# The second product of the larger experts with the weights stationary: output formed transposed, then turned over by transposes

## Chip, core and metric

One core of one Trainium2 chip runs the whole program. The metric is device time in microseconds (us) of one execution, lower is better. Engines are named as in the profile: PE (TensorE matmul), PEld (its weight loads), DVE (VectorE), ACT (ScalarE), POOL (GpSimd), SP (SyncE, which issues most of the DMAs).

## What is computed

An attention-like recurrence, a gated MLP, and a mixture of eight experts in which each of 3072 tokens goes to one expert. The change is in the last part:

```python
expert_idx = np.argmax(logits, axis=1)
gate_w = probs[np.arange(N), expert_idx]
for e in range(E):                       # E = 8, D = 384, F = 1024
    mask = expert_idx == e
    h = np.maximum(x[mask] @ w1[e], 0.0)
    out[mask] = gate_w[mask, None] * (h @ w2[e])
```

## The kernel before

The first 620 us compute the recurrence, the MLP and the routing. Each token's row (384 values, logits, its number) is scattered into `xs`, a region of slots for each expert. The last 245 us, the expert phase, is what the change touches.

Experts are taken by falling size. `CAPS` gives the slots of each: 448, 480, 448, 432, 416, 400, 384, 372. `tiles[e]` cuts them into row tiles: four when there are more than 384 slots (experts 0 to 5), else three. An expert has `XF` = 8 steps f, one for each 128 rows of the hidden layer. Every product is made of three matmuls on a high and a low part of the operands (32-bit data in a matmul format of reduced precision).

- `load_rows(e)` (L1168) brings the expert's rows from `xs` to `xrow`, by a DMA on SP. Its pool `xrp` has three buffers, so the load of expert e+2 takes the buffer of expert e-1. It is written into step 2 of expert e.
- `do_xT(e, k)` turns the rows into columns: transposes into a bank of `ps_t` (two banks), then a copy on ACT and a difference on DVE into `xk`.
- `load_we` and `split_we` bring the weights of one step (`wraw`, 384 KB, three buffers) by a DMA on SP and split them into `we`, high part on ACT (L816), low part on DVE (L819). `weights(e, f)` splits those of step f of the next expert and issues the load of the step two further on. `follow` keeps a split behind the last `relu` in `last_relu` in ACT's order.
- `emit_h(e, f)` (L1198): nine matmuls `ph` with the weights stationary and all slots as moving columns, into one of two banks; then `relu`: ACT (L902) and DVE (L903) write `ht`.
- `emit_y(e, f, t)` (L1211): for row tile t three matmuls `y` with the tile's columns of `ht` stationary (100 to 128 of them) and 384 columns of weights moving, summed over the eight steps into bank t of `ps_y`.
- `finish(e, t)` (L1222): the tile times its gate, on ACT for even t and on DVE for odd t, into `yo`, and a scatter by POOL (L1228) to the rows of `out` that `xrow` names. So the buffer `xrow` of an expert is free when its last scatter has landed.
- `drain2` (L1283) keeps `emit_y` two steps (`LAG`) behind `emit_h`: step 7 of expert e is drained in step 1 of expert e+1, and its tiles are finished there.

Expert 0 is treated apart (L1245 to L1279): its first 336 rows have been through `first_h` by then, and the last 112 go through short 32-bit matmuls (L1258) and `relu` into `h0`, between its `emit_y`.

The engines' queues run in order; a scheduler that works from its own estimates sets the order on each when the program is built, and an instruction waits in its queue for what it needs.

Of the kernel before, what the change touches and what calls it, by code (L numbers as in the profile page):

```python
# [8 lines left out]
F32 = mybir.dt.float32  # L9
# [5 lines left out]
AF = mybir.ActivationFunctionType  # L15
# [8 lines left out]
CAPS = (448, 480, 448, 432, 416, 400, 384, 372)  # L24
# [31 lines left out]
def kernel(  # L56
# [14 lines left out]
    nc = tc.nc  # L71
    P = 128
    NCH = att.shape[0]
    NT, DM = out.shape
# [5 lines left out]
    XF = 8  # L80
# [4 lines left out]
    wp = wstk.enter_context(tc.tile_pool(name="wp", bufs=18))  # L85
# [8 lines left out]
    def distinct_rows(key, ins):  # L94
        ins = getattr(ins, "ins", ins)
        tc.declare_no_dep(ins, group=key, reason="scatters of distinct rows")
        tc.add_to_no_dep_group(key, ins)
        scatters.setdefault(key, []).append(ins)
# [24 lines left out]
    def wtile(nm):  # L123
        return wp.tile([P, 1568], F32R, tag="w", name=nm)
# [169 lines left out]
    if True:  # L294
        ident = cst.tile([P, P], F32, name="ident")
# [159 lines left out]
        for i in range(7):  # L455
            n = 1 << i
# [4 lines left out]
        pt = ps_a.tile([P, 4, P], F32, tag="a0", name="pt")  # L461
# [339 lines left out]
        we = {}  # L801
# [9 lines left out]
        last_relu = []  # L811
# [81 lines left out]
        def products(ph, w, x):  # L893
            n = 0
            for k in range(3):
                wh, wl = w[:, k * P:(k + 1) * P], w[:, 768 + k * P:768 + (k + 1) * P]
                for a, b in ((wh, 0), (wh, 1), (wl, 0)):
                    nc.tensor.matmul(ph, a, x[:, k, b, :], start=(n == 0), stop=(n == 8))  # L898
                    n += 1

        def relu(ht, ph):
            q = nc.scalar.activation(ht[:, 0, :], ph, AF.Relu)  # L902
            nc.vector.scalar_tensor_tensor(ht[:, 1, :], ph, 0.0, ht[:, 0, :], op0=ALU.max, op1=ALU.subtract)  # L903
            return q
# [165 lines left out]
        while threads:  # L1070
            th = min((t for t in threads if met(t[3])), key=lambda t: t[0])
            now, t0, dt, need, name, gen = th
# [82 lines left out]
        ps_t = ph2.enter_context(tc.tile_pool(name="ps_t", bufs=2, space=bass.MemoryType.PSUM))  # L1155
        ps_y = ph2.enter_context(tc.tile_pool(name="ps_y", bufs=1, space=bass.MemoryType.PSUM))
# [3 lines left out]
        xk = {}  # L1160
        gate = {}
        hts = {}
        yo = {}


        tiles = [(c // (3 if c <= 3 * P else 4), 3 if c <= 3 * P else 4) for c in CAPS]

        def load_rows(e):  # L1168
            st, n = tiles[e]
            t = xrp.tile([st, n, RW], F32, tag="xrow", name="xrow", padded_shape=[P, 4, RW])  # L1170
            q = nc.sync.dma_start(
                out=t, in_=xs[bass.ds(at[e] * REGION, CAPS[e])].rearrange("(t p) c -> p t c", p=st)
            )
            after_scatters("xs", q)

            follow(getattr(q, "ins", q), last_we[0])
            xrow[e] = [t[:, i] for i in range(n)]
            xcol[e] = t[:, :, 384:393]

        def do_xT(e, k):  # L1180
            if k == 0:
                if e % 2 == 0:
                    t = r2p.tile([P, 3072], F32R, tag="r2", name="xk")
                else:
                    t = x2p.tile([P, 6 * REGION], F32R, tag="xk", name="xk")
                xk[e] = t[:, 0:6 * CAPS[e]].rearrange("p (k l n) -> p k l n", k=3, l=2)
            pt = ps_t.tile([P, CAPS[e]], F32, tag="t", name="pt2", padded_shape=[P, 512])
            st, n = tiles[e]
            for t in range(n):
                nc.tensor.transpose(pt[:, t * st:(t + 1) * st], xrow[e][t][:, k * P:(k + 1) * P], ident[:st, :st])  # L1190
            nc.scalar.activation(xk[e][:, k, 0, :], pt, AF.Copy)
            nc.vector.tensor_tensor(xk[e][:, k, 1, :], pt, xk[e][:, k, 0, :], op=ALU.subtract)

        def do_gate(e, after=None):
            x = xcol[e]
            gate[e] = gates(gp, *tiles[e], x[:, :, 0:E], x[:, :, E], after)

        def emit_h(e, f):  # L1198
            n = CAPS[e]
            ph = ps_h.tile([P, n], F32, tag="h", name="ph", padded_shape=[P, 512])  # L1200
            products(ph, we[e, f], xk[e])
            if e < E - 1:
                ht = hp.tile([P, 2 * REGION], F32R, tag="ht", name="ht")
            else:
                ht = wtile("ht")
            ht = ht[:, 0:2 * n].rearrange("p (l n) -> p l n", l=2)
            last_relu.append(relu(ht, ph))
            st, n = tiles[e]
            hts[e, f] = [ht[:, :, t * st:(t + 1) * st] for t in range(n)]

        def emit_y(e, f, t):  # L1211
            w = we[e, f]
            wh, wl = w[:, 384:768], w[:, 1152:1536]
            ht = hts[e, f][t]
            if f == 0:
                yo[e, t] = ps_y.tile([tiles[e][0], DM], F32, tag=f"y{t}", name=f"y{t}", padded_shape=[P, 512])
            for n, (a, b) in enumerate(((0, wh), (0, wl), (1, wh))):
                nc.tensor.matmul(  # L1218
                    yo[e, t], ht[:, a, :], b, start=(f == 0 and n == 0), stop=(f == XF - 1 and n == 2)
                )  # L1220

        def finish(e, t):  # L1222
            o = yp.tile([tiles[e][0], DM], F32, tag="yo", name="yo", padded_shape=[P, DM])
            if t % 2 == 0:
                nc.scalar.activation(o, yo[e, t], AF.Copy, scale=gate[e][:, t:t + 1])  # L1225
            else:
                nc.vector.tensor_scalar(o, yo[e, t], gate[e][:, t:t + 1], None, op0=ALU.mult)
            q = nc.gpsimd.indirect_dma_start(  # L1228
                out=out, out_offset=bass.IndirectOffsetOnAxis(ap=xrow[e][t].bitcast(I32)[:, 393:394], axis=0),
                in_=o, in_offset=None, bounds_check=NT - 1, oob_is_err=False,  # L1230
            )
            distinct_rows("out", q)
# [3 lines left out]
        def weights(e, f):  # L1236

            if e + 1 < E:
                n = (e + 1) * XF + f
                split_we(*todo[n])  # L1240
                if n + 2 < len(todo):
                    load_we(*todo[n + 2])
# [8 lines left out]
        pt = ps_t.tile([P, 3, ST], F32, tag="t", name="pt0")  # L1251
# [3 lines left out]
        for f in range(XF):  # L1255
            ph = ps_h.tile([P, ST], F32, tag="h", name="ph0")
            for k in range(3):
                nc.tensor.matmul(  # L1258
                    ph, fst["w", f // 4][:, f % 4, k * P:(k + 1) * P], x0T[:, k, :], start=(k == 0), stop=(k == 2)
                )  # L1260
            h0_done = relu(h0[:, f], ph)
            hm = fst["h", f // 2][:, f % 2]
            hts[0, f] = [hm[:, :, t * ST:(t + 1) * ST] for t in range(3)] + [h0[:, f]]
        c0 = fp.tile([ST, NST, 9], F32, name="c0")
# [3 lines left out]
        for f in range(XF):  # L1268
            for t in range(NST):
                emit_y(0, f, t)  # L1270
            weights(0, f)
            if 3 <= f < 6:
                do_xT(1, f - 3)
            elif f == 6:
                do_gate(0, h0_done if FIRST_AFTER else None)
                do_gate(1, h0_done if FIRST_AFTER else None)
                load_rows(2)
# [5 lines left out]
        def drain2(n):  # L1283
            while len(pend) > n:
                e, f = pend.pop(0)
                for t in range(tiles[e][1]):
                    emit_y(e, f, t)
                    if f == XF - 1:
                        finish(e, t)

        for e in range(1, E):
            for f in range(XF):
                emit_h(e, f)
                if e < E - 1:
                    pend.append((e, f))
                    weights(e, f)
                    if 3 <= f < 6:
                        do_xT(e + 1, f - 3)
                    elif f == 6:
                        do_gate(e + 1, last_relu[-1] if GATE_AFTER else None)  # L1300
                drain2(LAG)
                if f == 2 and e + 2 < E:
                    load_rows(e + 2)
        drain2(0)
        for t in range(tiles[E - 1][1]):
            for f in range(XF):
                emit_y(E - 1, f, t)
            finish(E - 1, t)
# [86 lines left out]
```

## Time and profile before

| | us |
|---|---|
| median of three runs (877.1 to 884.46) | 882.45 |
| profiled execution, its own time | 879.17 |
| its span, first to last instruction | 877.5 |
| expert phase in it: expert 0 up to the first `emit_h` of expert 1 | 618 to 653.1 |
| experts 1 to 7 | 653.1 to 864.8 |

The profiled execution is 3.3 us under the median of the runs. The profile lists busy time by engine, the chain of work that ended last, groups of instructions by line, and, by stretch of time, what each engine did and which clock TensorE was granted (1.00 is 2.4 GHz, 0.50 is 1.2 GHz). In a timeline a row merges like instructions: start, busy time, engine, line, operation, output and inputs, shape, count, and in brackets the idle time before it and what ended that.

### The profile page before, as it was taken

The numbers are of one execution on the slowest core, as the hardware profiler recorded it, in microseconds if no ns is written. First come the engines' busy times: TensorE is split into PE (matmuls) and PEld (weight loads), VectorE is DVE, ScalarE is ACT, GpSimd is POOL, SyncE is SP. The second block draws the span as 40 slices with busy tenths as digits, with TensorE's granted clock in tenths as the row PEclk, the third lists the DMA queues.
The fourth block names the chain that finished last, engine by engine and source line by source line (L and its number), as shares of the span: only waits on it lengthen the run. The fifth ranks groups of instructions, "written<-read, shape, count | busy, mean of one in ns | idle before, by whom it ended". The sixth has DMA issues, their size and how long they took to land.

```text
span 877.5 us, 13439 instructions
## 1 busy us (share of the span) xinstructions
PE 840.9 (96%) x5217; PEld 765.8 (87%) x5217; DVE 469.0 (53%) x950; ACT 328.3 (37%) x657; POOL 268.8 (31%) x297
## 2 busy tenths in 40 slices
PE   6898999899999999999999999999899999999994
PEld 5787988788888888888888888888899999999994
DVE  8988985645436444545455424343465554554640
ACT  4554543322224222422242214233354454453540
POOL 5504036755344634363435210200110201110111
PEclk9798999999999999999999999999999999999997
DMA  8716463222121212131213001520554445434401
GB/s 339 300 70 223 152 234 118 64 92 64 56 64 66 90 55 64 55 101 55 64 55 102 1 10 40 186 73 18 154 147 145 128 130 166 148 114 124 149 18 34
DMA packets 31865, 93.53 MB, mean 107 GB/s; under 512 B 4694, under 2 KB 15162, under 8 KB 28850
## 3 DMA queue, kind: packets, MB, share of 16 engines
q1 hardware_dynamic: 25010, 80.98, 27.5%
q0 software_dynamic: 6784, 11.61, 4.7%
q8 instruction: 43, 0.70, 0.3%
q14 instruction: 28, 0.23, 0.1%
HBM read 74.82 MB, written 16.25 MB: 104 GB/s over the span
## 4 chain that ended last, share of the span: by engine, by line
PE 82%; DVE 7%; issue 5%; ACT 2%; DMA 1%; POOL 1%; SPq 0%; POOLq 0%; ACTq 0%; DVEq 0%
PE o L750 18%; PE pgate L707 14%; PE pval L707 14%; PE y L1218 11%; PE ph L898 9%; PE pgv L707 4%; PE py L623 3%; PE pa L600 2%; PE py L619 2%; PE pg L431 1%; DVE x L401 1%; POOL out_dram L1228 1%; DVE x L402 1%; PE pt L1190 1%; DVE gt L739 1%
## 5 line engine op out<-in xcount | busy, mean ns | idle before, releaser
L707 PE MATMUL pgate<-xt,gv 128*128 128x512 f32 x540 | 136.0, 395 | 0.0
L707 PE MATMUL pval<-xt,gv 128*128 128x512 f32 x540 | 134.2, 393 | 0.0
L720 DVE TENSOR_TENSOR sgw<-pval,sgw 128x512 f32<-128x512 f32 x60 | 41.5, 691 | 162.1 <-PE pval L707 151.4
L750 PE MATMUL o<-wo,gth 128*128 128x392 f32 x480 | 126.6, 345 | 0.0
L707 PEld LDWEIGHTS pval<-xt,gv 128*128 128x128 f32 x540 | 100.3, 188 | 21.3
L1218 PE MATMUL y<-we,ht 128*120 128x384 f32 (+6 forms) x624 | 118.4, 339 | 0.0
L707 PEld LDWEIGHTS pgate<-xt,gv 128*128 128x128 f32 x540 | 100.8, 189 | 18.3
L898 PE MATMUL ph<-xk,we 128*128 128x336 f32 (+7 forms) x576 | 116.1, 349 | 0.0
L1218 PEld LDWEIGHTS y<-we,ht 128*120 128x120 f32 (+6 forms) x624 | 106.0, 175 | 2.6
L898 PEld LDWEIGHTS ph<-xk,we 128*128 128x128 f32 x576 | 102.7, 188 | 3.8 <-DVE ht L903 0.2
L561 POOL TENSOR_TENSOR Am<-ident,sd 128x1024 f32<-128x1024 f32 (+3 forms) x21 | 38.6, 1838 | 172.6 <-PE py L623 166.4
L716 ACT ACTIVATE sgw<-pgate 128x512 f32<-128x512 f32 x60 | 36.1, 601 | 141.6 <-PE pgate L707 141.6
L750 PEld LDWEIGHTS o<-wo,gth 128*128 128x128 f32 x480 | 85.8, 188 | 3.2 <-issue 0.5
L1228 POOL DMA_INDIRECT out_dram<-yo,xrow x26 | 28.7, 1103 | 181.2 <-ACT yo L1225 173.1
L750 PE MATMUL o<-wo,gtl 128*128 128x392 f32 x240 | 81.6, 340 | 0.0
L722 ACT ACTIVATE gth<-sgw 128x512 fp32r<-128x512 f32 x60 | 37.7, 629 | 97.9 <-DVE sgw L720 97.9
L903 DVE SCALAR_TENSOR_TENSOR ht<-ph,ht 128x480 fp32r<-128x480 f32 (+6 forms) x56 | 33.2, 592 | 73.9 <-ACT ht L902 73.6
L819 DVE TENSOR_TENSOR we<-wraw,we 128x768 fp32r<-128x768 f32 x64 | 61.2, 957 | 15.7 <-ACT we L816 11.8
L902 ACT ACTIVATE ht<-ph 128x480 fp32r<-128x480 f32 (+6 forms) x56 | 29.1, 520 | 96.3 <-PE ph L898 90.0
L724 DVE TENSOR_TENSOR gtl<-sgw,gth 128x512 fp32r<-128x512 f32 x60 | 48.9, 815 | 24.6 <-ACT gth L722 24.6
L707 PE MATMUL pgv<-xt,gv 128*128 128x256 f32 x432 | 59.9, 291 | 0.1
L816 ACT ACTIVATE we<-wraw 128x768 fp32r<-128x768 f32 x64 | 53.5, 838 | 14.6 <-DMA wraw<-in_wex_dram 10.6
(220 smaller groups left out, 1232.7 us busy)
## 6 DMA issues: line engine op xcount, KB each, us to landing
ld<-in_att_dram SPq DMA_DIRECT2D x23, 1152.0 KB, 5.6
wraw<-in_wex_dram SPq DMA_DIRECT2D x64, 384.0 KB, 3.0
raw<-in_wgv_dram SPq DMA_DIRECT2D x12, 768.0 KB, 10.5
xs<-zt SPq DMA_DIRECT2D x8, 750.0 KB, 6.9
raw<-in_wout_dram SPq DMA_DIRECT2D x6, 768.0 KB
xt<-xp POOLq DMA_DIRECT2D x60, 32.0 KB, 3.3
raw<-in_wex_dram SPq DMA_DIRECT2D x2, 768.0 KB
xrow<-xs SPq DMA_DIRECT2D x1, 750.0 KB
```

Source lines behind the costliest of these rows:

```text
L561: nc.gpsimd.tensor_tensor(Am[:, n:8], ident.unsqueeze(1).to_broadcast([P, 8 - n, P]), sd[c % 2][:, n:8].unsqueeze(2).to_broadcast([P, 8 - ...
L707: nc.tensor.matmul(pg, a, x[:, k, b, :], start=(n == 0), stop=(n == 8))
L716: nc.scalar.activation(sg, p0, AF.Sigmoid)
L720: nc.vector.tensor_tensor(sg, p1, sg, op=ALU.mult)
L722: nc.scalar.activation(hi, sg, AF.Copy)
L724: nc.vector.tensor_tensor(lo, sg, hi, op=ALU.subtract)
L750: nc.tensor.matmul(po[g][t], gt[a][:, ts_], w[:, f % 2, b, :], start=(f == 0 and n == 0), stop=(f == NF - 1 and n == 2))
L816: q = nc.scalar.activation(w[:, 0:768], r, AF.Copy)
L819: nc.vector.tensor_tensor(w[:, 768:1536], r, w[:, 0:768], op=ALU.subtract)
L898: nc.tensor.matmul(ph, a, x[:, k, b, :], start=(n == 0), stop=(n == 8))
L1218: nc.tensor.matmul(yo[e, t], ht[:, a, :], b, start=(f == 0 and n == 0), stop=(f == XF - 1 and n == 2))
L1228: q = nc.gpsimd.indirect_dma_start(out=out, out_offset=bass.IndirectOffsetOnAxis(ap=xrow[e][t].bitcast(I32)[:, 393:394], axis=0), in_=o, i ...
```

## The change

Experts 1 to 5, which have four tiles, form their output transposed: `emit_yT` takes each of three blocks of 128 weight columns as the stationary operand and moves all slots of the expert through it, nine matmuls a step in the place of twelve, into three banks of `ps_y`. After step 7 `evacuate_yT` copies the three banks to a buffer `yT` (blocks 0 and 2 on ACT, 1 on DVE; it takes one of the 18 buffers of the weights). In each of the steps 2 to 5 of the next expert `turn` transposes one row tile, three transposes into a bank of `ps_t`, and calls `finish` for it. Experts 0, 6 and 7 stay as they were. One more line puts the `relu` of `h0` into `last_relu`, so that in expert 0 the splits of expert 1's weights stand behind it on ACT.

```diff
+        def emit_yT(e, f):
+            w = we[e, f]
+            ht = hcol[e, f]
+            for m in range(3):
+                wh, wl = (w[:, o + m * P:o + (m + 1) * P] for o in (384, 1152))
+                if f == 0:
+                    yo[e, m] = ps_y.tile([P, CAPS[e]], F32, tag=f"y{m}", name=f"yT{m}", padded_shape=[P, 512])
+                for n, (a, b) in enumerate(((wh, 0), (wh, 1), (wl, 0))):
+                    nc.tensor.matmul(
+                        yo[e, m], a, ht[:, b, :], start=(f == 0 and n == 0), stop=(f == XF - 1 and n == 2)
+                    )
+
+        def evacuate_yT(e):
+            n = CAPS[e]
+            t = wp.tile([P, 1568], F32, tag="w", name="yT")[:, 0:3 * n].rearrange("p (m n) -> p m n", m=3)
+            yts[e] = t
+            for m in range(3):
+                if m == 1:
+                    nc.vector.tensor_copy(t[:, m], yo[e, m])
+                else:
+                    nc.scalar.activation(t[:, m], yo[e, m], AF.Copy)
+            turned.extend((e, i) for i in range(tiles[e][1]))
+
+        def turn():
+            e, t = turned.pop(0)
+            st = tiles[e][0]
+            pt = ps_t.tile([st, DM], F32, tag="t", name="pty", padded_shape=[P, 512])
+            for m in range(3):
+                nc.tensor.transpose(pt[:, m * P:(m + 1) * P], yts[e][:, m, t * st:(t + 1) * st], ident)
+            yo[e, t] = pt
+            finish(e, t)
...
             h0_done = relu(h0[:, f], ph)
+            last_relu.append(h0_done)
...
                 e, f = pend.pop(0)
+                if tiles[e][1] == 4:
+                    emit_yT(e, f)
+                    if f == XF - 1:
+                        evacuate_yT(e)
+                    continue
...
                 emit_h(e, f)
+                if turned:
+                    turn()
```

PE, where expert 1's last step meets the steps 1 and 2 of expert 2. Before (`y_6050` to `y_6062` are expert 1's four tiles, `y_6354` and on expert 2's):

```order
L898 MATMUL ph<-xk,we 128x448 x9
L1218 MATMUL y_6050<-we,ht 120x384 x3
L1218 MATMUL y_6054<-we,ht 120x384 x3
L1218 MATMUL y_6058<-we,ht 120x384 x3
L1218 MATMUL y_6062<-we,ht 120x384 x3
L898 MATMUL ph<-xk,we 128x448 x9
L1218 MATMUL y_6354<-we,ht 112x384 x3
```

Now:

```order
L898 MATMUL ph<-xk,we 128x448 x9
L1236 MATMUL yT_6050<-ht,we 128x480 x3
L1236 MATMUL yT_6054<-ht,we 128x480 x3
L1236 MATMUL yT_6058<-ht,we 128x480 x3
L898 MATMUL ph<-xk,we 128x448 x9
L1256 MATMUL pty<-ident,yT 120x128 x3
L1236 MATMUL yT_6322<-ht,we 128x448 x3
```

Nine matmuls in the place of twelve, and a tile's three transposes between `ph` of step 2 and the first product of the next expert.

ACT, from step 6 of expert 2 (448 slots) into the first steps of expert 3 (432 slots). Before:

```order
L902 ACTIVATE ht<-ph 128x448
L816 ACTIVATE we<-wraw 128x768
L131 ACT_TABLE_LOAD
L131 ACTIVATE gs<-xrow 108x4
L902 ACTIVATE ht<-ph 128x448
L816 ACTIVATE we<-wraw 128x768
L143 ACT_TABLE_LOAD
L143 ACTIVATE gl<-gl 108x32
L902 ACTIVATE ht<-ph 128x432
L816 ACTIVATE we<-wraw 128x768
L902 ACTIVATE ht<-ph 128x432
L816 ACTIVATE we<-wraw 128x768
```

Now:

```order
L902 ACTIVATE ht<-ph 128x448
L143 ACT_TABLE_LOAD
L143 ACTIVATE gl<-gl 108x32
L816 ACTIVATE we<-wraw 128x768 x3
L902 ACTIVATE ht<-ph 128x432
L816 ACTIVATE we<-wraw 128x768
L902 ACTIVATE ht<-ph 128x432
L816 ACTIVATE we<-wraw 128x768
L1248 ACTIVATE yT<-yT_6322 128x448
L1248 ACTIVATE yT<-yT_6330 128x448
L902 ACTIVATE ht<-ph 128x432
```

The splits of the steps 5, 6 and 7 of the next expert's weights, which stood one behind each `relu` in expert 2, stand in a row ahead of the first `relu` of expert 3, and the copies of `yT` stand behind two splits more. SP's order is the same as before: the load of `xrow` of expert e+2, then the loads of the weights.

ACT in expert 0, around the `relu` of `h0`. Before:

```order
L902 ACTIVATE hm<-ph_5641 128x336
L816 ACTIVATE we<-wraw 128x768 x2
L902 ACTIVATE hm<-ph_5653 128x336
L816 ACTIVATE we<-wraw 128x768
L902 ACTIVATE h_5723<-ph_5729 128x112
L902 ACTIVATE h_5723<-ph_5735 128x112
```

Now:

```order
L902 ACTIVATE hm<-ph_5641 128x336
L902 ACTIVATE hm<-ph_5653 128x336
L902 ACTIVATE h_5723<-ph_5729 128x112
L902 ACTIVATE h_5723<-ph_5735 128x112
L902 ACTIVATE h_5723<-ph_5741 128x112
L902 ACTIVATE h_5723<-ph_5747 128x112
```

The three splits have gone from ahead of `h0`'s first `relu`; all eight of expert 1's splits now stand behind its last.

## Rows read from the trace of the kernel before

**Rows 1.** The page's chain that ended last: share of the span by engine.

```profile
PE 82%; DVE 7%; issue 5%; ACT 2%; DMA 1%; POOL 1%; SPq 0%; POOLq 0%; ACTq 0%; DVEq 0%
```

**Rows 2.** Experts 1 to 7 by the view of stretches, with its column row.

```profile
core 0: us, PE busy (x) PEld busy (x) DVE busy (x) ACT busy (x) POOL busy (x), PEclk, DMA share, GB/s
653.10:864.60 211.50, 211.50 (x1195) 204.19 (x1194) 105.96 (x207) 96.08 (x160) 30.70 (x29) 1.00 0.40 121
```

**Rows 3.** Timeline of PE, steps without transposes: 480, 448 and 400 slots.

```profile
678.46 2.13 PE L898 MATMUL ph<-xk,we 128*128 128x480 f32 x9
680.43 2.27 PE L1218 MATMUL y<-we,ht 128*120 128x384 f32 x12
682.54 2.00 PE L898 MATMUL ph<-xk,we 128*128 128x448 f32 x9
684.38 2.29 PE L1218 MATMUL y<-we,ht 128*120 128x384 f32 x12
...
805.69 1.79 PE L898 MATMUL ph<-xk,we 128*128 128x400 f32 x9
807.32 2.26 PE L1218 MATMUL y<-we,ht 128*100 128x384 f32 x12
```

**Rows 4.** Timeline of PE around three transposes of 128 columns.

```profile
791.46 0.49 PE L1190 MATMUL pt<-ident,xrow 128*128 128x128 f32 x3
791.70 2.34 PE L1218 MATMUL y<-we,ht 128*100 128x384 f32 x12
793.88 1.79 PE L898 MATMUL ph<-xk,we 128*128 128x400 f32 x9
```

**Rows 5.** Expert 0: timelines of PE and ACT, then one stretch.

```profile
631.14 0.60 PE L1218 MATMUL y<-we,h 128*112 128x384 f32 x2 [2.33 <-ACT h L902]
630.09 0.84 ACT L816 ACTIVATE we<-wraw 128x768 fp32r<-128x768 f32 x1 [3.68 <-DMA wraw<-in_wex_dram]
632.00:636.00 4.00, 4.00 (x22) 3.84 (x21) 0.84 (x4) 1.16 (x3) 0.00 (x0) 0.57 0.31 103
```

**Rows 6.** SP's waits in the expert phase (total, times, longest); timelines of POOL and SP.

```profile
SPq L1171 <- DMA out_dram<-yo,xrow: 22.4, 7, 5.8
695.03 1.00 POOL L1228 DMA_INDIRECT out_dram<-yo,xrow  x1 [0.30 <-issue]
698.09 0.37 SPq L1171 DMA_DIRECT2D xrow<-xs  x1
793.62 0.31 SPq L1171 DMA_DIRECT2D xrow<-xs  x1
```

**Rows 7.** Stretches after the load of `xrow` at 698.09 (last: DMA share, GB/s); SP there.

```profile
704.00:706.00 2.00, 2.00 (x14) 1.86 (x14) 0.37 (x1) 0.94 (x2) 0.00 (x0) 1.00 0.93 356
706.00:707.00 1.00, 1.00 (x8) 0.99 (x7) 0.89 (x2) 0.75 (x2) 0.00 (x0) 1.00 0.19 73
707.00:708.00 1.00, 1.00 (x7) 0.95 (x6) 0.84 (x2) 0.00 (x0) 0.00 (x0) 1.00 0.00 0
...
703.04 8.98 SPq L807 DMA_DIRECT2D wraw<-in_wex_dram  x3
```

**Rows 8.** Timeline of ACT after the load of `xrow` at 793.62.

```profile
806.58 0.84 ACT L816 ACTIVATE we<-wraw 128x768 fp32r<-128x768 f32 x1 [6.33 <-DMA wraw<-in_wex_dram]
```

**Rows 9.** The page's DMA issues: KB each, median us from issue to landing.

```profile
wraw<-in_wex_dram SPq DMA_DIRECT2D x64, 384.0 KB, 3.0
```

**Rows 10.** Groups by shape, 715 to 748 us: busy us, mean ns of one, idle before.

```profile
L819 DVE TENSOR_TENSOR we<-wraw,we 128x768 fp32r<-128x768 f32 x9 | 8.6, 957 | 0.8
L816 ACT ACTIVATE we<-wraw 128x768 fp32r<-128x768 f32 x8 | 6.7, 838 | 0.0
L903 DVE SCALAR_TENSOR_TENSOR ht<-ph,ht 128x432 fp32r<-128x432 f32 x8 | 4.9, 607 | 12.8 <-ACT ht L902 12.8
L902 ACT ACTIVATE ht<-ph 128x432 fp32r<-128x432 f32 x8 | 4.2, 531 | 16.6 <-PE ph L898 14.1 <-issue 2.5
```

More of the change, by code (lines that the diff above doesn't have):

```diff
@@ L1162 @@
         hts = {}
+        hcol = {}
         yo = {}
@@ L1209, in emit_h @@
             hts[e, f] = [ht[:, :, t * st:(t + 1) * st] for t in range(n)]
+            hcol[e, f] = ht
         def emit_y(e, f, t):
@@ L1220, in emit_y @@
                 )
+        yts = {}
+        turned = []
+        def emit_yT(e, f):
[27 more added lines that the diff above has]
+            finish(e, t)
         def finish(e, t):
```

## Prediction

> **What bounds the kernel now.** I read the chain that ended last first: PE is most of it [rows 1]. Then the expert phase by stretches: from the first `emit_h` of expert 1 to the last product PE is busy 211.50 us of 211.50, at a granted clock of 1.00 (2.4 GHz) [rows 2]. So in experts 1 to 7 nothing but PE's own work sets the time, and a change there is worth what it takes out of PE's queue, as long as no other queue makes PE wait. Expert 0 is different: PE stood 2.33 us for the first `relu` of `h0`, because ACT stood 3.68 us at a weight split whose load had not landed [rows 5]. The timeline gives the price of a step by the distance of starts; the busy time of a merged row runs past the next start and is of no use for it.
>
> **What the product costs, and will cost.** Twelve `y` matmuls with 384 columns moving take 682.54 - 680.43 = 2.11 us [rows 3]. Nine matmuls with 128 stationary columns and all slots moving are exactly what `ph` is: 1.97 us at 480 slots, 1.84 at 448, 1.63 at 400 [rows 3]. The line between gives 1.77 at 432 and 1.70 at 416. So a step saves 0.14, 0.27, 0.34, 0.41 and 0.48 us in the experts 1 to 5, together 1.64, and over eight steps **13.1 us**. The wider weight load costs nothing here, since `ph` has it too.
>
> **What the turning costs PE.** A turn is three transposes of 128 columns. The same three were put in by `do_xT` of expert 6: 0.24 us from the first to the next `y` [rows 4], and the `y` step behind them takes 793.88 - 791.70 = 2.18, 0.07 more than without [rows 3]. That is 0.31 us a turn, and 20 turns are **6.2 us**. PE's own work thus falls by **6.9 us**.
> By the Trainium skill ("TensorE: Matmul & The Clock Gate", Part 4: PE-mode transpose) a 128x128 transpose took about 275 ns in a kernel's context; 60 of them would be 16.5 us by that figure, more than the products save. [rows 4] show some 0.1 us each in this kernel.
>
> **Expert 0.** Expert 1's eight splits now stand behind the last `relu` of `h0`, so ACT no longer holds `h0` up for a load. The wait of 2.33 us goes, and with it the slow stretch behind it: the granted clock was 0.57 on average from 632 to 636 [rows 5], which is 4 x 0.43 = 1.7 us of PE time. Of the 4.0 us some comes back, because the short matmuls of `h0` have two banks and each must pass ACT and DVE before the next but one starts; I take **-3.5 us**, between -2 and -4. Late next are the splits themselves: they start some 9 us later, but PE still has about 16 us of expert 0's products then, and the first `emit_h` needs one of them alone.
>
> **What the turning moves on the other queues.** The copies of `yT` (15, each about as long as a `relu` of as many columns, 0.53 us on ACT and 0.61 on DVE [rows 10]) and the 20 `finish` fit: ACT and DVE are busy 96 and 106 us of 211.5 [rows 2]. What I do not price at nothing is the place of the scatters. `finish` of expert e-1 ran in step 1 of expert e; now its tiles are turned in the steps 2 to 5. POOL has nothing else queued. But the load of `xrow` for expert e+2 waits on SP for those scatters [rows 6], and queued behind it on SP are the weight loads. Today they wait 22.4 us in all, mostly hidden [rows 6]. Now the load goes out four steps later, the splits of the last three steps of the next expert's weights have moved into one row on ACT behind it, and `relu`, two more splits and the copies of `yT` stand behind those. The first turn waits for the copies, PE for the turn.
>
> I walk this chain for expert 2, from the start of expert 1's fourth turn (0). Transposes 0.3, `finish` on DVE 0.6, scatter to the issue of `xrow` 698.09 - 695.03 = 3.1 [rows 6], three hand-overs some 0.8 (an estimate): `xrow` goes out at X = 4.8. In the trace an `xrow` issued at 698.09 and three weight loads behind it, the third issued at 703.04, kept the DMA streaming until 706 to 707 and then nothing moved [rows 7]: the third lands about X + 9.1, the ones ahead of it 1 us apart. A buffer of `wraw` is free after split and difference, 0.84 + 0.96 [rows 10], and a load alone lands in 3.0 [rows 9], so the fourth and fifth land at X + 7.1 + 1.8 + 3.1 = X + 12.0 and X + 13.0. On ACT the fourth split ends at X + 12.9, a `relu` at 13.4, the fifth split at 14.2; DVE's difference at 15.2 and its copy of `yT` at 15.8. The first turn of expert 2 can start at 20.6. PE gets there after a turn and four transposes (0.7), five products of expert 2 and two `ph` (7 x 1.84) and three `ph` of expert 3 (3 x 1.77): 18.9. **PE waits 1.7 us.**
> For expert 3 the chain is the same and PE's way shorter (0.7 + 7 x 1.77 + 3 x 1.70 = 18.2): 2.4. Expert 4's `xrow` is smaller; between nothing and 3 I take 1.
> Expert 5 is the bad one. Behind the `xrow` of expert 7 (372 slots) ACT got its first weights 806.58 - 793.62 = 13.0 us after the issue [rows 6, 8]. In the old order ACT's 6.33 us at that split cost PE nothing [rows 2, 8]; now two splits in a row stand ahead of expert 6's first `relu`. They end on ACT at X + 14.9, on DVE at 15.8, and DVE's part of the `relu` at 16.4, which is 21.2. PE stands at `ph` of step 2 (the bank is not free) from 0.6 + 7 x 1.63 + 2 x 1.58 = 15.2, so it waits 6.0; and again before the turn, for two more splits (loads at X + 17.9 and 18.9) and two copies, until 25.6 against 22.8: 2.8.
> Together 1.7 + 2.4 + 1 + 8.8 = **13.9 us** of new waits; the bounds are 0 (all loads land in time) and some 20 (each link 1 us later).
>
> **The clock.** The wait of 2.33 us was followed by a granted clock at its lower level, 1.7 us lost [rows 5]. Three of the new waits are about as long or longer: 3 x 1.7 = 5.1, of which expert 5's falls partly into its second wait. I take **+4**, between 0 and 7.
>
> **The sum** against the profiled execution's 879.17 us (span 877.5): -6.9 - 3.5 + 13.9 + 4 = +7.5, **887 us**. The median of the runs shown is 3.3 above that execution, so a median may stand at 890; I put the forecast between, at 888.
>
> **Rivals.**
> 1. *The waits do not appear.* For it: PE lost nothing to ACT's 6.33 us before, `emit_y` lags two steps, there are two `ph` banks. Against: the copies of `yT` are a new link that has no such slack. Then -6.9 - 3.5 = -10.4: 869 against the profiled execution, 872 against the median. It decides if the chain for expert 2 is under 18.9 us, and the first split behind expert 7's `xrow` comes 6 us sooner than before.
> 2. *Only expert 5 waits.* Experts 2 to 4 miss by 1 to 2.4 us, which is within what the walk can tell. Then -10.4 + 8.8 + 1 = -0.6: 879, no change.
> 3. *The turns cost PE more than the transposes of `do_xT`.* A turn reads what ACT and DVE have just written, and if nothing of it overlaps with its neighbours, its three transposes take their whole busy time, 0.49 [rows 4]: 20 x 0.18 = 3.6 more, 891 with the waits, 873 without. Against it: the `pt` of [rows 4] stand between the same kinds of matmuls and do overlap. By the page's 275 ns it would be 10.3 more, 897 with the waits.
>
> **How the numbers follow.** Forecast 0.56, rival 1 0.14, rival 2 0.22, rival 3 0.08. A measurement of this kernel tells about 1% (8.8 us) from no change. Of the forecast's 0.56 I put 0.39 above that bound and 0.17 within, as the sum lies near it and both the waits and the clock can run higher. Rival 2 is within 1%, rival 1 faster, rival 3 half within and half above. So faster 0.14, same 0.43, slower 0.43. The range runs from rival 1 against the median, 872, to the waits 6 us larger and the median's offset, 900.
>
> **What the profile after would show.** Nine matmuls `yT` a step, 1.97 to 1.63 us from start to start; turns of 0.3 us; expert 0 without ACT's wait for `wraw` and without a low clock behind it; SP's `xrow` of the experts 4 to 7 some four steps later than before; PE idle before `pty` of the experts 2 to 5, released by a copy of `yT`, and before `ph` of expert 6, with a lower clock behind. I am wrong if PE runs through these places, if the loads behind `xrow` land much sooner than [rows 7, 8] say, or if transposes cost more than 0.1 us.

## The result, and the profile after

The changed kernel took 884.8 us (median of 20 runs, 879.77 to 889.88) against 879.86 us before (20 runs, 875.42 to 884.46). The ratio is 1.0053, with a 95% interval of 1.0033 to 1.0074: some 4.7 us or 0.5% slower. That is within the 1% that was put as the bound of "same", yet clear of no change. The forecast was 888, in a range of 872 to 900.

The profiled execution after has a span of 886.7 us, before 877.5. Not all of these 9.2 us are the change's. Expert 0's first transposes stood at 625.34 us before and stand at 628.90 now, behind 620 us of the same program; in the nine profiles of the experiments that point lies between 623.4 and 631.3 us. So the first 3.6 us come and go from one execution to the next, and the comparison has to be made from that point on. It falls into two stretches.

The first is expert 0, from those transposes to expert 1's first `ph`. PE's timeline of the kernel before has (start, us, line, operation, out<-in, count, and later the idle time before):

```profile
625.34 0.45 PE L1253 MATMUL pt<-ident,x 112*128 112x112 f32 x3
```

and that of the kernel after:

```profile
628.90 0.45 PE L1291 MATMUL pt<-ident,x 112*128 112x112 f32 x3
...
633.32 0.41 PE L1220 MATMUL y<-we,h 128*112 128x384 f32 x1
...
652.62 6.01 PE L898 MATMUL ph<-xk,we 128*128 128x480 f32 x27
```

That is 653.1 - 625.3 = 27.8 us before [rows 2] and 652.6 - 628.9 = 23.7 now: **-4.1 us**. PE's wait of 2.33 us in front of the first `y` on `h` [rows 5] is gone: the row at 633.32 has no idle time in front of it. ACT runs the splits behind the last `relu` of `h0`, without a wait for their load (timeline of ACT, after):

```profile
636.91 2.30 ACT L816 ACTIVATE we<-wraw 128x768 fp32r<-128x768 f32 x3
```

The second stretch is experts 1 to 7, up to the last matmul. The view of stretches, after (us, then busy time and count of PE, PEld, DVE, ACT, POOL, the granted clock, DMA share, GB/s):

```profile
652.60:873.90 221.30, 211.53 (x1136) 199.63 (x1134) 108.22 (x212) 102.06 (x170) 28.75 (x29) 0.97 0.40 119
```

211.5 us have become 221.3: **+9.8 us**, although PE has 59 instructions less in it (1136 for 1195). PE's busy time of 211.53 is no larger than before [rows 2], but PE is idle for 221.30 - 211.53 = 9.8 us where it had not stood at all [rows 2], and the granted clock is 0.97 where it was 1.00. The busy time hides the saving, since matmuls at the lower clock count as busy for about twice as long (below, nine `ph` for 3.25 us in place of 1.75); over the whole span PE is busy for 842.9 us after and 840.9 before, with 60 instructions less.

The waits of 652 to 875 us name the places (engine, tile and line, waited for; us in total, times, longest). These are PE's three lines and ACT's one for loads:

```profile
ACT we L816 <- DMA wraw<-in_wex_dram: 18.9, 11, 7.5
...
PE ph L898 <- DVE ht L903: 4.8, 1, 4.8
...
PE pty L1256 <- ACT yT L1248: 3.4, 4, 1.4
...
PE pty L1256 <- DVE yT L1246: 1.6, 3, 0.8
```

PE waits for the copies of `yT` ahead of a turn seven times, 5.0 us, and once for 4.83 us ahead of `ph`. SP's own waits, 650 to 850 us, show where this begins: the load of `xrow` now stands 65.0 us behind the scatters that must leave its buffer, where it had stood 22.4 [rows 6].

```profile
SPq L1172 <- DMA out_dram<-yo,xrow: 65.0, 8, 13.1
```

In time the load is not four whole steps late, as the prediction had it, but some 10 us, about two and a half steps: `xrow` of expert 4 goes out 707.62 - 652.62 = 55.0 us into the stretch, where it had been 698.09 - 653.1 = 45.0 [rows 6]. Before, the four scatters of an expert stood one behind the other on POOL (from 690.65 to 695.03), so the last of them was late as well.

From expert 2 to 3 it reads so in the timelines (SP, ACT, PE, DVE, after): the load of `xrow` goes out, the weight loads behind it, two splits stand one behind the other on ACT and each waits for its load, the copies of `yT` come behind them, and PE's turn waits for one copy of ACT and one of DVE.

```profile
707.62 0.37 SPq L1172 DMA_DIRECT2D xrow<-xs  x1
...
719.14 0.85 ACT L816 ACTIVATE we<-wraw 128x768 fp32r<-128x768 f32 x1 [1.62 <-DMA wraw<-in_wex_dram]
...
721.21 0.85 ACT L816 ACTIVATE we<-wraw 128x768 fp32r<-128x768 f32 x1 [0.80 <-DMA wraw<-in_wex_dram]
721.96 0.96 ACT L1248 ACTIVATE yT<-yT 128x448 f32<-128x448 f32 x2
...
722.54 0.32 PE L1256 MATMUL pty<-ident,yT 128*112 128x128 f32 x1 [0.22 <-ACT yT L1248]
...
722.96 0.62 DVE L1246 COPY yT<-yT 128x448 f32<-128x448 f32 x1
...
723.64 0.43 PE L1256 MATMUL pty<-ident,yT 128*112 128x128 f32 x2 [0.78 <-DVE yT L1246]
723.82 2.01 PE L1236 MATMUL yT<-ht,we 128*128 128x432 f32 x9
```

The same two rows of `pty` read 1.38 and 0.39 us after expert 3, and 0.48 and 0.41 after expert 4. After expert 5 the load is that of expert 7's 372 slots, and ACT stands 7.48 us at a split, with a `relu` of expert 6 behind it (timelines of the same engines; the first row is the fourth turn of expert 4, from which the prediction's walk counts):

```profile
799.93 0.49 PE L1256 MATMUL pty<-ident,yT 128*104 128x128 f32 x3
...
804.33 0.31 SPq L1172 DMA_DIRECT2D xrow<-xs  x1
...
813.53 1.79 PE L1236 MATMUL yT<-ht,we 128*128 128x400 f32 x9
816.81 1.83 ACT L816 ACTIVATE we<-wraw 128x768 fp32r<-128x768 f32 x2 [7.48 <-DMA wraw<-in_wex_dram]
...
819.55 0.55 DVE L903 SCALAR_TENSOR_TENSOR ht<-ph,ht 128x384 fp32r<-128x384 f32 x1
...
820.15 3.25 PE L898 MATMUL ph<-xk,we 128*128 128x384 f32 x9 [4.83 <-DVE ht L903]
...
824.68 0.88 PE L1256 MATMUL pty<-ident,yT 128*100 128x128 f32 x3 [1.28 <-ACT yT L1248]
```

The nine matmuls of `ph` then take 3.25 us, where 1.75 was the rule. The stretches give the granted clock (third number from the end) at expert 2's wait, after expert 3's, and at and after expert 5's:

```profile
720.00:724.00 4.00, 3.00 (x16) 2.35 (x15) 3.39 (x5) 2.54 (x5) 0.00 (x0) 1.00 0.58 198
756.00:760.00 4.00, 3.61 (x13) 3.22 (x12) 2.06 (x4) 1.66 (x3) 1.00 (x1) 0.59 0.55 177
816.00:820.00 4.00, 0.00 (x0) 0.00 (x0) 2.29 (x3) 3.04 (x5) 0.00 (x0) 0.77 0.19 65
820.00:824.00 4.00, 3.25 (x9) 2.74 (x9) 2.88 (x5) 1.58 (x3) 0.00 (x0) 0.50 0.79 264
824.00:828.00 4.00, 3.32 (x12) 3.17 (x13) 2.47 (x3) 2.72 (x6) 0.99 (x1) 0.50 0.68 197
```

0.50 is the lower level of 1.2 GHz. After the waits of the experts 2 and 4 the clock stays at 1.00.

### The profile page after: what moved, and what is told of

The parts are those of the page before. It is cut to its first block, busy times and chain, and to the rows that moved or that the text cites. A ratio compares the mean times of both kernels' runs of the same rounds, so it can differ in the third digit from the quotient of the medians.

```text
span 886.7 us, 13326 instructions
## 1 busy us (share of the span) xinstructions
PE 842.9 (95%) x5157; PEld 763.0 (86%) x5157; DVE 470.6 (53%) x955; ACT 334.7 (38%) x667; POOL 267.1 (30%) x297
## 4 chain that ended last, share of the span: by engine, by line
PE 62%; issue 22%; DVE 7%; POOL 3%; ACT 2%; DMA 2%; POOLq 0%; SPq 0%; ACTq 0%
PE o L750 17%; PE pgate L707 14%; PE pval L707 14%; PE pgv L707 4%; POOL out_dram L1266 3%; PE py L623 2%; PE pa L600 2%; PE py L619 2%; PE ph L898 1%; PE pg L431 1%; DVE x L402 1%; DVE x L401 1%; DMA xrow<-xs 1%; PE pa L577 1%; DMA ld<-in_att_dram 1%
## 5 line engine op out<-in xcount | busy, mean ns | idle before, releaser
L898 PEld LDWEIGHTS ph<-xk,we 128*128 128x128 f32 x576 | 105.0, 191 | 9.4 <-DVE ht L903 5.2
L1266 POOL DMA_INDIRECT out_dram<-yo,xrow x26 | 26.7, 1028 | 192.9 <-ACT yo L1263 158.5
L1236 PE MATMUL yT<-ht,we 128*128 128x480 f32 (+4 forms) x360 | 80.8, 368 | 0.0
L1236 PEld LDWEIGHTS yT<-ht,we 128*128 128x128 f32 x360 | 66.7, 191 | 3.5
L707 PE MATMUL pgv<-xt,gv 128*128 128x256 f32 x432 | 62.6, 300 | 0.1
L707 PEld LDWEIGHTS pgv<-xt,gv 128*128 128x128 f32 x432 | 59.9, 206 | 1.1 <-DVE xt L685 0.4
```

Source lines behind the costliest of these rows:

```text
L707: nc.tensor.matmul(pg, a, x[:, k, b, :], start=(n == 0), stop=(n == 8))
L1236: nc.tensor.matmul(yo[e, m], a, ht[:, b, :], start=(f == 0 and n == 0), stop=(f == XF - 1 and n == 2))
L1266: q = nc.gpsimd.indirect_dma_start(out=out, out_offset=bass.IndirectOffsetOnAxis(ap=xrow[e][t].bitcast(I32)[:, 393:394], axis=0), in_=o, i ...
```

## The experiments

Each run below is timed beside the kernel before on the same chip; the ratio is to that kernel.

**A fourth buffer for `xrow`.** If the time is lost because the load of `xrow` waits for scatters that now come later, a free buffer lets it go out at once. Nothing else of the change is touched, and SP's loads keep their order.

```diff
-        xrp = ph2.enter_context(tc.tile_pool(name="xrp", bufs=3))
+        xrp = ph2.enter_context(tc.tile_pool(name="xrp", bufs=4))
```

> The changed kernel with four buffers for xrow in the place of three; nothing else. Theory (the load of xrow waits on SP for the scatters of the turned tiles, holds up the weight loads behind it, and so the splits, the copies of yT and PE): SP's wait is gone, PE runs from the first product of expert 1 to the last without waiting and at the full clock, that stretch takes 211.5 - 6.9 = 204.6 us, and the time is 884.8 - 16.6 = 868. Rival (the turns themselves cost PE, by their own copies and transposes): the waits before pty stay, time 880 to 885.

Measured: 869.36 us (867.22 to 872.44), before 880.36; ratio 0.9869 (0.9829 to 0.9908). The stretch of experts 1 to 7 in this kernel:

```profile
647.50:852.60 205.10, 205.10 (x1135) 195.99 (x1134) 107.71 (x212) 101.23 (x170) 28.75 (x29) 1.00 0.44 130
```

No idle PE, the clock at 1.00, and 16.2 us less than after. No load of `xrow` waits for the scatters any more, and ACT waits for loads 1.6 us in all. The whole loss of the changed kernel comes from that one wait for a buffer. This is also the clean view of what the change does to PE: 211.5 to 205.1, or -6.4 us. Steps read in PE's timeline of this kernel:

```profile
681.63 2.12 PE L1236 MATMUL yT<-ht,we 128*128 128x480 f32 x9
683.59 2.02 PE L898 MATMUL ph<-xk,we 128*128 128x448 f32 x9
685.46 0.49 PE L1256 MATMUL pty<-ident,yT 128*120 128x128 f32 x3
685.70 2.08 PE L1236 MATMUL yT<-ht,we 128*128 128x448 f32 x9
687.61 1.99 PE L898 MATMUL ph<-xk,we 128*128 128x448 f32 x9
```

A product of 480 slots takes 683.59 - 681.63 = 1.96 us (2.11 before [rows 3]). A turn is 685.70 - 685.46 = 0.24 to the next product, and that product 687.61 - 685.70 = 1.91, against 1.84 without transposes [rows 3]: 0.31 in all.

**The load of `xrow` five steps later.** The other way to take the wait off SP's queue: ask for the rows where the scatters are already done, so that the weight loads go ahead of them.

```diff
-                if f == 2 and e + 2 < E:
+                if f == 7 and e + 2 < E:
```

> The changed kernel with the load of xrow of expert e+2 written into step 7 of expert e in the place of step 2; still three buffers. Theory: the scatters have landed by then, SP does not wait, and the weight loads of the steps 3 to 7 go out ahead of it; most of the 16.6 us comes back, except that the slow load for expert 7 (13 us until the weights behind it) now meets the first steps of expert 6: 869 to 875. Rival (turns cost by themselves): 880 to 885.

Measured: 867.13 us (866.57 to 868.31); ratio 0.9838 (0.9794 to 0.9881). The same stretch:

```profile
647.50:852.60 205.10, 205.10 (x1135) 196.03 (x1134) 107.62 (x212) 101.11 (x170) 28.71 (x29) 1.00 0.44 129
```

The same stretch as with four buffers (from the first `ph` to the last matmul the two differ by about 0.01 us), with three. It beat the 869 to 875 that were expected: the slow load of expert 7's rows now stands behind all of expert 6's weights on SP, ahead of the last six loads, which are expert 7's, and costs PE nothing. What the load must not do is stand in front of weights that are due.

**Without the line for `h0`.** This undoes the part of the change that moves expert 1's splits.

```diff
-            last_relu.append(h0_done)
```

> The changed kernel without the line that puts the relu of h0 into last_relu. Theory: expert 0 is as before, with ACT at a split of which the load has not landed and 2.3 us of waiting and a low clock on PE; 884.8 + 4.1 = 889. Rival (the line is worth nothing, since the wait moves elsewhere): 885.

Measured: 890.26 us (887.84 to 894.28); ratio 1.0108 (1.007 to 1.0147), 0.0055 above the changed kernel's. ACT's and PE's waits are back, as in [rows 5]; ACT's timeline of this kernel:

```profile
629.08 0.84 ACT L816 ACTIVATE we<-wraw 128x768 fp32r<-128x768 f32 x1 [3.63 <-DMA wraw<-in_wex_dram]
```

and PE's:

```profile
630.13 0.98 PE L1220 MATMUL y<-we,h 128*112 128x384 f32 x2 [2.28 <-ACT h L902]
```

Expert 0 takes 652.14 - 624.39 = 27.75 us, and experts 1 to 7 are as in the changed kernel (221.1 for 221.3). The two parts of the change do not touch each other.

**That line alone, in the kernel before.**

```diff
             h0_done = relu(h0[:, f], ph)
+            last_relu.append(h0_done)
```

> The kernel before with that line alone. Theory: 4.1 less than before, 875.8, with expert 0 shorter by about 4 us from its first transpose to the first ph of expert 1. Rival: no change, 879.9.

Measured: 877.34 us (874.68 to 881.63); ratio 0.9962 (0.9935 to 0.9989). Expert 0 gained its 4.1 us, but 1.1 came back in experts 1 to 7 (212.6 for 211.5), in one place, at `ph` of expert 6 behind the slow load (timeline of PE):

```profile
805.14 1.86 PE L898 MATMUL ph<-xk,we 128*128 128x384 f32 x9 [1.02 <-DVE ht L903]
```

So even in the old order PE was close to a wait there: ACT's 6.33 us at that split [rows 8] were hidden, with little to spare.

**Each turn's transposes twice.** On top of the fourth buffer, so that no wait blurs it: 60 more transposes, each written a second time to the same place (the output is the same). This prices them by themselves.

```diff
-            for m in range(3):
+            for m in (0, 1, 2) * 2:
```

> The kernel with four xrow buffers, each turn's three transposes issued twice into the same bank: 60 more. Theory (a transpose of 128 columns costs PE 0.107 us between these products, as a turn of three costs 0.31 to 0.32): 869.4 + 6.4 = 876. Rival (the Trainium skill's 0.275 us each, 'TensorE: Matmul & The Clock Gate', Part 4): 869.4 + 16.5 = 886.

Measured: 877.2 us (874.63 to 882.88), before 878.79; ratio 0.998 (0.9955 to 1.0005). The stretch of experts 1 to 7:

```profile
649.20:860.80 211.60, 211.60 (x1195) 202.56 (x1194) 107.70 (x212) 101.07 (x170) 34.26 (x29) 1.00 0.43 126
```

211.6 - 205.1 = 6.5 us for 60, **0.108 us each**, with PE still busy throughout. By the 275 ns of the Trainium skill ("TensorE: Matmul & The Clock Gate", Part 4: PE-mode transpose) it would have been 16.5, the rival's estimate. The page gives the figure for bf16 in one kernel; as the length of one transpose the trace agrees with it: 272 ns in the median (count, then shortest, median and longest in ns).

```profile
L1256 PE MATMUL pty<-ident,yT x120: 270/272/275, 687.1 to 824.6; 128*120 128x128 f32 x24, 128*112 128x128 f32 x24, 128*108 128x128 f32 x24, 128*104 128x128 f32 x24
```

But one transpose overlaps with the next, so the length of one is not what one more costs PE; the distance of starts is.

**The last expert with 384 slots in place of 372.** How much of the loss is the slow load of expert 7's rows? 384 slots are three tiles of 128 rows, where 372 are three of 124.

```diff
-CAPS = (448, 480, 448, 432, 416, 400, 384, 372)
+CAPS = (448, 480, 448, 432, 416, 400, 384, 384)
```

> The changed kernel, three xrow buffers, with room for 384 slots in place of 372 in expert 7: its rows are then three tiles of 128 partitions instead of 124. Theory (of the time lost after expert 1 the larger half is the slow load of expert 7's rows, 11 to 13 us until the weights behind it): the wait before ph of expert 6 goes (4.8 us), the low clock behind it too (about 3), the experts 2 to 4 wait as before; products of expert 7 cost 0.4 more, the last scatters land some 2 us sooner: 884.8 - 9 = 876. Rival (the slow load is slow for what is in flight beside it, not for its shape): 884 to 885.

Measured: 878.66 us (874.56 to 884.96), before 878.79; ratio 0.9993 (0.9961 to 1.0025). The same stretch of this kernel:

```profile
650.50:863.20 212.70, 207.19 (x1136) 195.85 (x1134) 108.38 (x212) 102.76 (x170) 28.11 (x29) 1.00 0.42 126
```

8.6 of the 16.2 us are gone with 12 slots more to compute, and 9 were expected. By the medians the gain is 6.1 us (878.66 for 884.8); the first 620 us alone vary by more than is missing. The load still goes out late, but ACT gets its weights soon after it, and PE's wait at `ph` of expert 6 does not appear. SP's timeline of this kernel:

```profile
801.83 0.38 SPq L1172 DMA_DIRECT2D xrow<-xs  x1
```

and ACT's:

```profile
807.19 1.82 ACT L816 ACTIVATE we<-wraw 128x768 fp32r<-128x768 f32 x2 [0.36 <-DMA wraw<-in_wex_dram]
```

807.19 - 801.83 = 5.4 us, against 816.81 - 804.33 = 12.5 in the changed kernel. What stays are the waits for the copies of `yT`, in the experts 2 to 5 (its waits):

```profile
PE pty L1256 <- ACT yT L1248: 3.9, 4, 1.5
...
PE pty L1256 <- DVE yT L1246: 1.6, 3, 0.8
```

With 384 slots and no waits the stretch takes 205.5 us (the next run), 0.4 of it for the 12 slots. So the loss splits into some 9.0 us for the slow load and 212.7 - 205.5 = 7.2 for the four waits that stay. That is good to a microsecond or two, since the waits that stay are not the same to the tenth in both runs, and the clock did not fall behind expert 3's here.

**Both: rows late, and 384 slots.**

```diff
-CAPS = (448, 480, 448, 432, 416, 400, 384, 372)
+CAPS = (448, 480, 448, 432, 416, 400, 384, 384)
...
-                if f == 2 and e + 2 < E:
+                if f == 7 and e + 2 < E:
```

> Rows loaded in step 7 and 384 slots in expert 7. Theory: no waits are left to remove, so only the last scatters gain, 867.1 + 0.4 - 2 = 865.5. Rival (the last scatters are late for another reason than their 124 partitions): 867.5.

Measured: 872.46 us (867.83 to 874.91); ratio 0.9912 (0.9878 to 0.9945). A miss: it should have been as fast as the late rows alone, or faster. Its profile has experts 1 to 7 in 205.5 us without idle PE:

```profile
652.80:858.30 205.50, 205.50 (x1135) 196.36 (x1134) 107.62 (x212) 101.23 (x170) 28.00 (x29) 1.00 0.44 130
```

It has an end that is 0.3 us shorter where 2 were expected, but expert 0 begins at 629.06 us and not at 623.77 as with the late rows alone, so 5.3 us lie in the first part, which both kernels share. Since that point varies by itself, the two were run again side by side, with the same edits. First the late rows alone:

> The kernel with rows loaded in step 7 once more, now on the same chip as the one with 384 slots. Theory (the 5 us between the two came from the first 620 us, where the two programs are the same): both within 1 us of each other, 867 to 870. Rival (384 slots cost time): 867 against 872.

Measured: 869.29 us (867.25 to 874.63), before 879.29; ratio 0.9874 (0.9844 to 0.9905). Then the late rows with 384 slots:

> The kernel with rows loaded in step 7 and 384 slots in expert 7, once more beside the other. Theory: within 1 us of it, with equal time from the first transpose of expert 0 on. Rival: 5 us slower.

Measured: 870.76 us (870.23 to 875.2); ratio 0.991 (0.9877 to 0.9942). The medians differ by 1.5 us, a little more than expected, and the intervals overlap: 384 slots bring nothing that can be measured once the rows are asked for late. The version with the rows late measured 0.9838 and 0.9874, the one with a fourth buffer 0.9869; their intervals overlap, so neither is shown to be the faster, and both beat the kernel before and the changed one.

## Why the prediction was right

The forecast's sign, its size (+7.5 by the sum; +5.7 between the two profiles from expert 0 on; +4.7 timed) and its mechanism held. The time alone would not have told it from rival 2's "no change": the prediction put 0.39 of its 0.56 on more than 1%, and the measured 0.5% lies between the two. The waits in the profile, and the two runs that take them away, decide. The 888 also held a part of an offset of 3.3 us from a median of three runs; with twenty runs that offset is 0.7 (879.86 - 879.17). By the prediction's own steps:

- **What PE's own work loses:** predicted -6.9, measured 205.1 - 211.5 = -6.4 where no wait is in the way. Turns 6.2 predicted, 6.5 measured for 60 transposes; so products, by subtraction, -12.9 for -13.1. The distances of starts in [rows 3, 4] gave both within 5%.
- **Expert 0:** predicted -3.5, measured -4.1, by undoing the line and by doing it alone. Nothing of the 4.0 came back inside `h0`.
- **The new waits:** predicted 13.9, measured 9.8 of idle PE. All four experts wait, each for what the walk named, and in the order of size that it gave: 1.0 for 1.7 (expert 2), 1.8 for 2.4 (expert 3), 0.9 for 1 (expert 4), 4.8 + 1.3 for 6.0 + 2.8 (expert 5). This is the **term that was mis-sized**, by 4.1, chiefly at expert 5. There four small errors all went the same way: `xrow` went out 804.33 - 799.93 = 4.4 us after the fourth turn and not 4.8; the first split began 816.81 - 804.33 = 12.5 us behind it and not 13.0; DVE's part of the `relu` ended at 820.10, 3.3 us behind that and not 3.4; and PE came to `ph` at 813.53 + 1.79 = 815.3, 15.4 us after the turn and not 15.2. Of the second wait's 2.8, 1.5 went by inside the slow `ph` (3.25 - 1.75).
- **Starting again:** not in the sum. A turn that waits also costs PE some 0.4 us that are neither idle time nor lower clock. In the run with 384 slots PE stands 5.5 us (212.7 - 207.19) and the granted clock is 1.00, yet the stretch is 7.2 us longer than with the rows late: 1.7 us more, at four waits. In the rows of expert 2 above, the turn takes 723.82 - 722.54 - 0.78 = 0.50 us to the next product without its idle time, where 0.24 is the rule: its transposes no longer overlap with their neighbours. That is what rival 3 feared for all 20 turns; it came true for four.
- **The clock:** predicted +4, between 0 and 7. What is left of the loss is 221.3 - 205.1 - 9.8 = 6.4, and without 1.7 for starting again 4.7. The stretches say the same: PE was busy for 3.61 us at 0.59 (756 to 760) and for 3.25 + 3.32 at 0.50 (820 to 828), so it lost 3.61 x 0.41 + 6.57 x 0.50 = 4.8. The size was right, but not for the reason given, some 1.7 a wait: expert 3's wait was followed by a slow stretch of about the size of expert 0's, expert 2's and 4's by none, and expert 5's by one of some 10 us. Nor does the length of a wait settle it: in the run with 384 slots expert 3's waits are as long (1.8 us), and the clock stays at 1.00.

```profile
752.00:756.00 4.00, 2.21 (x13) 1.58 (x12) 3.66 (x6) 3.41 (x6) 0.00 (x0) 1.00 0.59 185
756.00:760.00 4.00, 4.00 (x26) 3.91 (x25) 1.59 (x4) 1.65 (x3) 1.50 (x2) 1.00 0.34 126
```

Waits, starting again and the clock together are 16.2 for 17.9, and the fourth buffer took away exactly these. The waits came out too long, starting again was left out, and the clock's size did not come from its rule; that the sum is closer than its terms is partly luck.

**Rival 1** (the waits do not appear) and **rival 2** (only expert 5 waits) fell for this kernel: PE waits in all four experts. The split of the loss into 9.0 and 7.2 says that rival 2 would have been some 7 us off. Rival 1 is what the changed kernel becomes with a buffer more or the load later, and its -10.4 is then -6.4 - 4.1 = -10.5 by the profiles (867 to 869 timed, for 869 to 872). **Rival 3** (turns dearer than `do_xT`'s transposes) fell by the turns written twice: 0.108 us each, and one turn reads 0.31. Only the four turns that waited cost more.

One view misled if read alone. The page's chain that ended last fell from 82% PE [rows 1] to this, after:

```profile
PE 62%; issue 22%; DVE 7%; POOL 3%; ACT 2%; DMA 2%; POOLq 0%; SPq 0%; ACTq 0%
```

That looks like the waits, but the kernel with the fourth buffer, where PE never stands in experts 1 to 7, has 63% and 21% there. The stretches and the waits of one stage told the truth.

## What to carry to other kernels

When work that ends in a scatter moves to later steps, follow the buffer that the scatter frees: a load that waits for it holds up every load queued behind it, and here that turned a saving of 10.5 us into a loss of 5, until one buffer more, or a later place in the queue, gave it back. Price the matmuls by distances of starts, but walk the queue's chain as well, and do not trust the result to better than a microsecond or two: a wait is the difference of two long chains, and here one such wait came out 6.1 us in place of 8.8. Time saved on an engine is worth only as much as the engine's stage shows; compare stages, since 620 us of the same program here differed by up to 8 us between executions.

## What the runs showed of the hardware that was not expected

Loads and scatters of tiles of 124 rows were far slower than those of 128. Behind the load of 3 x 124 rows the first weights reached ACT 12.5 us after its issue, behind 3 x 128 rows 5.4 us. While the 124 rows streamed, the 16 DMA engines were as busy as under the load of expert 6's 3 x 128 rows, issued at 774.09, yet moved 217 GB/s and not 363 (stretches of the changed kernel, the last two numbers):

```profile
808.00:812.00 4.00, 4.00 (x24) 4.00 (x24) 0.93 (x4) 1.32 (x2) 0.00 (x0) 1.00 1.04 217
776.50:779.50 3.00, 3.00 (x18) 2.98 (x17) 1.84 (x9) 2.06 (x4) 0.00 (x0) 1.00 1.03 363
```

The scatters show it within one run. In the first run with the rows late, the three scatters of expert 6's tiles of 128 rows landed in 2.6 us (median) and were 64 packets each; the three of expert 7's tiles of 124 rows, right behind them, landed in 6.2 us and were 192 packets each. The DMA view of that run, 838 to 845.4 and 845.4 to 860 us (packets, MB and share of the scatters' queue, then the issues):

```profile
q0 software_dynamic: 192, 0.55, 19.8%
...
out_dram<-yo,xrow POOLq DMA_INDIRECT x3, 2.6
...
q0 software_dynamic: 576, 0.51, 15.4%
...
out_dram<-yo,xrow POOLq DMA_INDIRECT x3, 6.2
```

It is not that 124 are fewer than 128: in the same run the scatters of 120, 112, 108, 104 and 100 rows landed in 2.7 to 3.8 us, with 64 packets each, and 80 at 100 rows. Why 124 rows stand apart was not tried.

Even so the program's end, from the last matmul on, gained only 0.3 us by 128 rows; what else holds the end was not tried.
